# DeltaNet followed by soft MoE: the separate solve of the keys is taken out of each step, and the order is planned with other durations

## The chip, the cores and the metric

The kernel runs on one core of one Trainium2 chip. The metric is the device time of one execution in microseconds (us). A core has five engines that run beside each other, each through its own list of instructions in order: PE (TensorE, matrix products), DVE (VectorE), ACT (ScalarE), POOL (GpSimd) and SP (SyncE, which here only starts transfers). PE writes its results to PSUM, eight banks of 128 partitions by 512 floats; DVE and ACT bring them from there to SBUF.

## What is computed

The first half is a recurrent attention: for each of 4 x 8 pairs of batch and head, a state of 48 x 48 is carried through 768 positions. The second half routes the 3072 resulting rows through 8 experts with 4 slots each. Everything is float32.

```python
# attention: q, k, v (4, 8, 768, 48), beta (4, 8, 768)
k_n = k / (np.linalg.norm(k, axis=-1, keepdims=True) + 1e-06)
for t in range(S):
    y[:, :, t] = np.einsum('bhd,bhde->bhe', q[:, :, t], state)
    v_old = np.einsum('bhde,bhd->bhe', state, kt)
    state = state + bt[:, :, :, None] * np.einsum('bhd,bhe->bhde', kt, vt - v_old)
# soft MoE: x = y as (3072, 384), phi (384, 32), w1 (8, 384, 1024), w2 (8, 1024, 384)
logits = x @ phi
d = softmax of logits over the rows;  c = softmax of logits over the slots
slot_input = d.T @ x
h = np.maximum(slot_input[e] @ w1[e], 0.0);  slot_out[e] = h @ w2[e]
return c @ slot_out
```

## The kernel before, in words

The 768 positions are cut into 24 chunks ("steps", n = 0 to 23) of 32 positions; four batches of 32 positions fill the 128 partitions. Four steps make a group (m = 0 to 5). Inside a chunk the recurrence is a triangular system: with T the inverse of a unit lower triangular matrix built from the products of the chunk's keys, the chunk's update is W = T (V - K S), where S is the state on entry, K the keys and V the values.

Work that does not depend on the state, per group: loads of K, Q and V by SP; `turn` (L508, PE transposes of K and Q; ACT copies them to X at L518); `products` (L536, key by key and key by query; evicted to G at L549 and L553 and to AT at L557); `invert`, which makes T for the whole group (DVE transposes of 128x1024 at L574 and L670, 28 short POOL instructions at L653 and L657, two PE blocks at L701 and L706, and ACT's two scaled copies into DTb at L622); and `scale_v` (L725, POOL).

Work of one step, `chain(n)`, from step 1 on. One bank or pair of banks is taken for each product:

- KP, the solve of the keys (L755, PE, 16 products of 64x64): T K into two banks of the kind "bulk"; then an ACT copy of 128x512 with scale -1 (L764) overwrites the keys' half of X with it. It needs DTb and K, not the state.
- VP, the solve of the values (L773, PE): T V into two "chain" banks `hw`. It needs DTb, the scaled V and, by an explicit key, KP's copy, but not the state.
- R (L787, PE): -(T K) S is added to the same banks. It needs the state St.
- QS (L743, PE): Q S into a bank `hy`. It needs St.
- W: half of `hw` is spread into W by a DVE instruction (L799) and the other half by two of ACT (L804); ACT also makes the plain copy Wc (L808).
- S (L817, PE): K^T W is added to the state, which stays in two PSUM banks of its own; ACT (two of L827) and DVE (L831) copy it to St for the next step.
- AU (L842, PE) adds the chunk's inner part to `hy`, and ACT evicts it to Y (L848).

So the loop from state to state is R, W, S, St, and then R of the next step; KP and VP lie ahead of it.

After each group, `route` makes the logits and the running softmax sums (L866 to L950); after the last, `experts` runs the two expert layers (L1118, L1137, L1156) and the final product and stores (L1200 to L1220). The experts' weights are loaded by SP into the buffers of the first half as these come free (L1010). Rings of buffers: V has 6 slots, and SP's load of V for a later step (L476) waits until the last reader of the slot is done, which is VP of an earlier step.

The order in which each engine issues its work is written by a planner, `Plan`. Every `plan.op` gives an engine, a duration in us, what it reads and writes, and which PSUM banks it takes and frees. `order()` runs a list scheduling: at each moment it takes the operation of greatest worth, which is the length of the longest way to the end plus a correction by name from the table `BIAS` (the suffixes 0 and 5 stand for the first and last group). Six of the eight banks are shared; at most four may be held by "bulk" work. A model of the PE clock and of code fetching (`BLOCK`, `FETCH`) is part of it, and idle PE time may be filled with throw-away products (L466). The durations are estimates written in the code: `act(n)`, `dve(n)`, `pool(n)`, `pe(...)` or a plain number. The order is fixed when the program is made; on the chip each engine follows it and waits where something is late.

Of the kernel before, what the change touches and what calls it, by code (L numbers as in the profile page):

```python
# [10 lines left out]
ALU = mybir.AluOpType  # L11
ACT = mybir.ActivationFunctionType
# [5 lines left out]
    "ACT.DTb": 1.7, "ACT.DTb0": 0.8, "ACT.DTb5": -9.4, "ACT.G": 105.2, "ACT.G0": -5.0,  # L18
    "ACT.G5": 33.6, "ACT.Gl": 0.7, "ACT.Gl0": -20.9, "ACT.Gl5": -14.9, "ACT.KP": 3.6,
    "ACT.KP5": 56.7, "ACT.S": 17.6, "ACT.S5": 3.7, "ACT.W": -10.0, "ACT.W5": 13.1, "ACT.Wc":  # L20
    -4.6, "ACT.Wc5": 37.2, "ACT.X": -13.0, "ACT.X0": -8.8, "ACT.Y": 4.1, "ACT.Y5": 1.8,
    "ACT.al5": -6.7, "ACT.cT5": -37.8, "ACT.dT": 6.6, "ACT.gmax": 15.8, "ACT.hT": -23.0,
    "ACT.hr": 5.5, "ACT.lT5": 11.3, "ACT.norm": -15.2, "ACT.norm0": 21.2, "ACT.norm5": 5.9,
    "ACT.ob": 27.7, "ACT.share": -15.9, "ACT.share5": 2.6, "ACT.store": -8.0, "ACT.yT": 3.3,
    "ACT.yT5": -5.6, "DVE.AT": -15.1, "DVE.AT5": -27.5, "DVE.DT": -7.3, "DVE.DT-": 10.1,
    "DVE.DT-0": 23.8, "DVE.DT-5": -5.6, "DVE.DT0": -33.9, "DVE.DT5": -16.3, "DVE.DTb0": 60.8,
    "DVE.Dn5": 7.9, "DVE.G": -35.8, "DVE.G0": -2.5, "DVE.G5": 4.8, "DVE.N": -3.5, "DVE.N0":
    -14.4, "DVE.N5": 10.9, "DVE.S": 3.9, "DVE.S5": 24.7, "DVE.W": 4.4, "DVE.W5": -0.8,
    "DVE.X16": 17.4, "DVE.X160": -26.6, "DVE.X165": -14.0, "DVE.elim0": -28.1, "DVE.hT": 11.4,
    "DVE.lb": 86.8, "DVE.lb0": 35.6, "DVE.lb5": 14.0, "DVE.low0": 5.7, "DVE.low5": -18.5,  # L30
    "DVE.masks": -15.7, "DVE.max": 0.7, "DVE.max5": 13.4, "DVE.norm": 1.0, "DVE.norm0": -2.7,
    "DVE.norm5": -95.2, "DVE.ob": -6.6, "DVE.rd": 15.5, "DVE.sacc": 10.5, "DVE.sacc5": -13.5,
    "DVE.share5": -6.7, "DVE.sj": 5.0, "DVE.sl": -33.3, "DVE.so": -18.2, "DVE.ssq0": 32.2,
    "DVE.tD0": -62.5, "DVE.tS0": 3.1, "DVE.zero": 0.2, "PE.AU": -7.5, "PE.AU5": -5.2, "PE.KP":
    6.9, "PE.QS": -22.2, "PE.QS5": 3.8, "PE.R": -2.4, "PE.S": -0.1, "PE.S5": -14.4, "PE.T16":
    -9.8, "PE.T165": 12.8, "PE.VP": 8.8, "PE.VP5": 2.1, "PE.X16": 18.2, "PE.X160": -5.0,
    "PE.X165": -34.9, "PE.cT": -0.9, "PE.gather": 41.6, "PE.gmax": 1.1, "PE.logits": 14.4,
    "PE.logits5": 5.6, "PE.po": -0.1, "PE.prod": -5.8, "PE.prod0": -2.0, "PE.prod5": 3.0,
    "PE.second": 15.7, "PE.slots": 0.5, "PE.slots5": -4.4, "PE.turn": 4.5, "PE.turn0": -2.1,
    "PE.turn5": 33.5, "PE.turnD": 7.9, "PE.turnD5": 6.7, "PE.turnH": -15.5, "PE.turnL": 2.7,  # L40
    "PE.turnL5": 11.0, "PE.turnY": 42.7, "POOL.Dn2": 1.6, "POOL.Dn20": -6.1, "POOL.Dn25": 10.0,
    "POOL.elim": -6.7, "POOL.elim5": 0.8, "POOL.loadB0": 19.5, "POOL.loadP0": -10.4,
    "POOL.masks": 8.2, "POOL.one": 23.8, "POOL.one0": -19.4, "POOL.one5": 3.6, "POOL.scaleV":
    24.0, "POOL.scaleV5": 1.9, "POOL.share": -36.1, "POOL.share5": -22.5, "POOL.tD": -9.2,
    "POOL.tD5": -51.3, "POOL.tS": 20.2, "POOL.tS5": -4.9, "POOL.zero": 8.0, "SP.loadK0": 3.9,
    "SP.loadK5": 4.9, "SP.loadQ": -5.8, "SP.loadQ0": -88.6, "SP.loadV": -79.9, "SP.loadV0":
    43.4, "SP.loadV5": -4.8, "SP.loadW": 19.9, "SP.store": 4.3,
# [15 lines left out]
class Plan:  # L63
# [10 lines left out]
    BLOCK, FETCH, LAND = 128, 3.5, 2.3  # L74
# [240 lines left out]
def kernel(  # L315
# [39 lines left out]
    def buf(shape, name):  # L355
        return cpool.tile(shape, F32, name=name)
# [29 lines left out]
    Wc = [Wcall[:, i].rearrange("p (h d) -> p h d", d=D) for i in range(2)]  # L386
    St = buf([P, B, HQ, 2, D], "St")
# [24 lines left out]
    def act(n):  # L412
        return 0.22 + 0.00082 * n

    def dve(n, ps=False, per=1.04):
        return 0.035 + (0.15 if ps else 0.16) + n * per / 1000
# [106 lines left out]
    def products(n, which):  # L523
# [20 lines left out]
        for o, i in enumerate(which):  # L544
            ps = lambda o=o: at(h, 0, 2)[:, :, 0:2 * w * C * HQ].rearrange(
                "p g (e o t) -> p g e o t", e=HQ, o=w)[:, :, :, o, :]
            if i == 0:
                dst = G[m % 2][:, H * c:H * c + H].rearrange("p (e g) t -> p g e t", g=2)
                plan.op("ACT", act(256), lambda ps=ps, dst=dst: nc.scalar.activation(  # L549
                    dst, ps()[:, :, :, 0:C], ACT.Copy, scale=par[:, 0:1]), r=[h],  # L550
                    w=[("G", m % 2, c)], rel=h, name="G")
                for g in range(2):
                    D_(dve(128, True), lambda ps=ps, dst=dst, g=g: nc.vector.scalar_tensor_tensor(  # L553
                        dst[:, g], ps()[:, g, :, C:2 * C], par[:, 1:2], dst[:, g], op0=ALU.mult,
                        op1=ALU.add), r=[h, ("G", m % 2, c)], w=[("G", m % 2, c)], rel=h, name="G")
            else:
                D_(dve(512, True), lambda ps=ps: nc.vector.tensor_tensor(  # L557
                    AT[n % NA], ps(), tri.rearrange("p j t -> p (j t)").unsqueeze(1).unsqueeze(1)
                    .broadcast_to([P, 2, HQ, 2 * C]), op=ALU.mult),
                   r=[h], w=[("AT", n % NA)], rel=h, name="AT")  # L560
# [4 lines left out]
    def invert(m):  # L565
# [50 lines left out]
        for j in range(2):  # L616
# [4 lines left out]
            else:  # L621
                plan.op("ACT", act(1024) + 0.08, lambda j=j: nc.scalar.activation(  # L622
# [3 lines left out]
    def invert_joined(m, z, gr, gm, gk):  # L626
# [32 lines left out]
        for j in range(1, QC - 1):  # L659
            for part in range(2):  # L660
                n = 2 * j * (QC - 1 - j)
                plan.op(on, 0.31 + 1.72 * n / 1000 if m else dve(n, False, 0.86),
# [21 lines left out]
        for j in (1, 0):  # L684
            plan.op("POOL", 0.72, lambda j=j: nc.gpsimd.tensor_tensor(
# [3 lines left out]
        for j in range(2):  # L689
            plan.op("ACT", act(512), lambda j=j: nc.scalar.activation(  # L690
# [43 lines left out]
    def chain(n):  # L734
# [13 lines left out]
        hy, hw, hk = Banks(1, "chain"), Banks(2, "chain"), Banks(2, "bulk")  # L748
        if n:
            def solve_keys():  # L750
                for e in range(HQ):
                    for i in range(2):
                        for g in range(2):
                            rb = slice(2 * C * i, 2 * C * i + 2 * C)
                            nc.tensor.matmul(  # L755
                                at(hk, i)[DP * g:DP * g + DP, 2 * C * e:2 * C * e + 2 * C],
                                lhsT=kk[rb, 2 * e + g, :],
                                rhs=t[rb, H * c + 2 * e + g].rearrange("p j t -> p (j t)"),
                                start=(e == 0), stop=True, skip_group_check=True)

            plan.op("PE", pe(16, 64, 64, 4, 0.25), solve_keys,
                    r=[("DTb", m % 2, j) for j in range(2)] + all4("K", n % NK), w=[hk], acq=hk,
                    pre=[("X", n % NX, 0)], name="KP")
            plan.op("ACT", act(512), lambda: nc.scalar.activation(  # L764
                x[:, 0].rearrange("p e (i t) -> p i e t", i=2),
                at(hk, 0, 2)[:, :, 0:2 * C * HQ].rearrange("p i (e t) -> p i e t", e=HQ), ACT.Copy,
                scale=-1.0), r=[hk], w=[("X", n % NX, 0)], rel=hk, name="KP")

        def solve():
            for u in range(H):  # L770
                for i in range(2):
# [3 lines left out]
                                     rhs=vn[rb, u, :], start=(u % HQ == 0), stop=True,  # L775
# [3 lines left out]
                r=[("DTb", m % 2, j) for j in range(2)] + [("V", n % NV), ("X", n % NX, 0), "turns"],  # L779
                w=[hw], acq=hw, name="VP")  # L780
        if n:
            def shift():
                for e in range(HQ):
                    for b in range(B):
                        rb = slice(C * b, C * b + C)
                        e2 = 2 * D * (e % 2)
                        nc.tensor.matmul(at(hw, e // 2)[rb, e2:e2 + 2 * D], lhsT=x[:, 0, e, rb],  # L787
                                         rhs=St[:, b, e].rearrange("p g d -> p (g d)"),
                                         start=False, stop=True, skip_group_check=True)

            plan.op("PE", pe(16, 32, 96, 4, 0.25), shift,
                    r=[("X", n % NX, 0)] + sk, w=[hw, "turns"], bias=LOOP, name="R")
            plan.op("PE", pe(16, 32, 96, 4, 0.25), lambda: state(hy, 1),
                    r=[("X", n % NX, 1)] + sk, w=[hy], acq=hy, pre=[("Y", m % 2, c)], name="QS")

# [7 lines left out]
        for j in range(2):  # L803
            plan.op("ACT", act(192), lambda j=j: nc.scalar.activation(  # L804
# [53 lines left out]
    def route(m):  # L858
# [73 lines left out]
        plan.op("ACT", act(128), lambda: nc.scalar.activation(  # L932
# [94 lines left out]
    def experts():  # L1027
# [164 lines left out]
        for m in range(NG):  # L1192
# [14 lines left out]
            for s in range(2):  # L1207
# [8 lines left out]
                for x in range(2):  # L1216
# [3 lines left out]
                    plan.op(on, 0.5, lambda o=o, x=x, dst=dst, on=on: queues[on][0].dma_start(  # L1220
                            out=dst, in_=ob[o][0][DP * x:DP * x + DP]),
                        r=[("ob", o)], w=[("out", m, s, x)], land=0.55, name="store")
# [66 lines left out]
```

## Time and profile before

| | |
|---|---|
| median of 3 runs | 320.19 us (319.81 to 324.7) |
| profiled execution | 322.18 us; span of its trace 320.4 us |
| mean granted PE clock | 0.949 |
| PE / DVE / ACT / POOL busy | 273.6 / 167.0 / 156.5 / 107.0 us |
| PE busy from 44 to 274 us (windows view) | 210.0 of 230 us |
| KP: PE block L755, ACT copy L764 | 23 blocks, 17.1 us busy; 23 copies, 13.7 us busy |

The span is the time from the first to the last instruction of one profiled execution. It falls into three parts: up to about 44 us the first loads and the first group's inverse; from 44 to 274 us the steps, the other groups' inverses and the routing, all interleaved; from 274 us the experts and the stores. A row of the groups view gives the line, engine and shape of an instruction, how often it ran, its busy time, the mean duration of one, and how long its engine stood idle just before it. Each fp32 matrix product stands in the trace as two instructions, so a block of 16 products is 32 records. The records of neighbouring PE blocks overlap, since PE is pipelined; what a block occupies is read from its start to the start of the next. The chain of work goes back from the last instruction, at each step to what released it.

### The profile page before, as it was taken

The numbers are of one execution on the slowest core, as the hardware profiler recorded it, in microseconds if no ns is written. First come the engines' busy times: TensorE is split into PE (matmuls) and PEld (weight loads), VectorE is DVE, ScalarE is ACT, GpSimd is POOL, SyncE is SP. The second block draws the span as 40 slices with busy tenths as digits, with TensorE's granted clock in tenths as the row PEclk, the third lists the DMA queues.
The fourth block names the chain that finished last, engine by engine and source line by source line (L and its number), as shares of the span: only waits on it lengthen the run. The fifth ranks groups of instructions, "written<-read, shape, count | busy, mean of one in ns | idle before, by whom it ended". The sixth has DMA issues, their size and how long they took to land.

```text
span 320.4 us, 16406 instructions
## 1 busy us (share of the span) xinstructions
PE 273.6 (85%) x7296; PEld 223.1 (70%) x7296; DVE 167.0 (52%) x363; ACT 156.5 (49%) x325; POOL 107.0 (33%) x239
## 2 busy tenths in 40 slices
PE   3849797998997898999988999998898988999840
PEld 3739686887877797789867888787787875444410
DVE  7699992487345195445952648736231345220530
ACT  2542174637646357456485566853174765020330
POOL 9922148522872018830088400784000000000000
PEclk9987999899999799999999999999599999999995
DMA  5665544544444555544134660678677789595197
GB/s 96 101 108 83 96 79 72 92 66 77 78 73 83 85 86 86 81 69 79 23 91 88 126 210 5 166 179 304 222 210 239 219 256 359 162 407 202 50 302 237
DMA packets 88933, 45.25 MB, mean 141 GB/s; under 512 B 80016, under 2 KB 80144, under 8 KB 88864
## 3 DMA queue, kind: packets, MB, share of 16 engines
q1 hardware_dynamic: 86752, 42.69, 53.2%
q10 hardware_dynamic: 1568, 1.38, 1.4%
q8 instruction: 57, 0.93, 1.2%
q0 software_dynamic: 544, 0.15, 0.4%
q14 instruction: 12, 0.10, 0.1%
HBM read 39.47 MB, written 4.72 MB: 138 GB/s over the span
## 4 chain that ended last, share of the span: by engine, by line
PE 61%; DVE 14%; POOL 7%; issue 5%; DMA 5%; ACT 4%; SPq 0%; ACTq 0%; DVEq 0%; POOLq 0%
PE bank L842 7%; PE bank L536 6%; PE bank L743 5%; PE bank L773 5%; PE bank L817 5%; PE bank L787 5%; PE bank L508 4%; PE bank L755 3%; PE bank L1118 3%; PE bank L1156 3%; PE bank L701 3%; PE bank L706 3%; POOL bt L497 3%; PE bank L866 2%; DVE DT L670 2%
## 5 line engine op out<-in xcount | busy, mean ns | idle before, releaser
L518 ACT ACTIVATE X<-bank 128x512 f32<-128x512 f32 (+1 forms) x36 | 25.9, 739 | 32.1 <-PE bank L508 32.1
L725 POOL TENSOR_TENSOR Vall<-Vall,nT 128x384 f32<-128x384 f32 x24 | 19.8, 830 | 61.5 <-DMA Vall<-in_v_dram 29.9
L536 PE MATMUL bank<-X 48*64 48x64 f32 (+1 forms) x1152 | 32.9, 258 | 5.7 <-ACT X L518 5.3
L831 DVE TENSOR_TENSOR St<-bank,half 128x768 f32<-128x768 f32 x23 | 22.0, 955 | 26.3 <-PE bank L817 15.0
L536 PEld LDWEIGHTS bank<-X 48*64 48x64 f32 x1152 | 27.7, 149 | 10.5 <-ACT X L518 7.3
L827 ACT ACTIVATE St<-bank 48x384 f32<-48x384 f32 x46 | 22.3, 484 | 22.1 <-PE bank L817 12.9
L553 DVE SCALAR_TENSOR_TENSOR G<-bank,par,G 128x128 f32<-128x128 f32 x48 | 14.5, 342 | 28.4 <-ACT G L549 28.4
L773 PE MATMUL bank<-Vall,DTb 64*64 64x48 f32 x768 | 28.0, 222 | 0.6 <-issue 0.5
L842 PE MATMUL bank<-Wcall,ATall 64*64 64x48 f32 x768 | 27.6, 221 | 0.3 <-issue 0.3
L773 PEld LDWEIGHTS bank<-Vall,DTb 64*64 64x64 f32 x768 | 25.6, 138 | 3.2 <-issue 1.2
L842 PEld LDWEIGHTS bank<-Wcall,ATall 64*64 64x64 f32 x768 | 25.7, 138 | 1.7 <-issue 1.0
L657 POOL TENSOR_TENSOR tt<-tt,prPOOL 128x28 f32<-128x28 f32 (+6 forms) x70 | 24.7, 353 | 5.2
L804 ACT ACTIVATE W<-bank,par 128x192 f32<-128x192 f32 x48 | 17.5, 416 | 18.2 <-PE bank L787 17.4
L508 PE MATMUL bank<-ident,Kall 128*128 128x128 f32 x96 | 17.5, 319 | 9.5 <-DMA Kall<-in_k_dram 7.1
L653 POOL TENSOR_TENSOR prPOOL<-tt 128x28 f32<-128x28 f32 (+6 forms) x70 | 23.7, 339 | 5.0
L817 PE MATMUL bank<-W,Kall 64*48 64x96 f32 x736 | 22.6, 251 | 2.5 <-issue 1.9
L743 PE MATMUL bank<-St,X 128*32 128x96 f32 x736 | 22.7, 259 | 2.2 <-issue 1.6
L787 PE MATMUL bank<-St,X 128*32 128x96 f32 x736 | 20.8, 250 | 1.4 <-ACT St L827 0.8
L799 DVE TENSOR_TENSOR W<-bank,par 128x384 f32<-128x384 f32 x24 | 13.2, 550 | 15.9 <-PE bank L787 13.4
L817 PEld LDWEIGHTS bank<-W,Kall 64*48 64x48 f32 x736 | 17.5, 123 | 5.1 <-issue 3.4
L557 DVE TENSOR_TENSOR ATall<-bank,tri 128x512 f32<-128x512 f32 x24 | 16.4, 685 | 8.5 <-PE bank L536 8.1
L743 PEld LDWEIGHTS bank<-St,X 128*32 128x32 f32 x736 | 16.8, 114 | 5.6 <-issue 3.7
(212 smaller groups left out, 572.1 us busy)
## 6 DMA issues: line engine op xcount, KB each, us to landing
Vall<-in_v_dram SPq DMA_DIRECT2D x96, 48.0 KB, 2.6
Qall<-in_q_dram SPq DMA_DIRECT2D x96, 48.0 KB, 2.6
Kall<-in_k_dram SPq DMA_DIRECT2D x92, 48.0 KB, 2.5
X<-in_moe_w_dram SPq DMA_DIRECT2D x6, 512.0 KB, 4.6
X<-in_moe_w_dram SPq DMA_DIRECT2D x7, 384.0 KB, 5.6
Kall<-in_moe_w_dram SPq DMA_DIRECT2D x3, 512.0 KB, 5.0
Kall<-in_moe_w_dram SPq DMA_DIRECT2D x4, 384.0 KB, 5.6
ATall<-in_moe_w_dram SPq DMA_DIRECT2D x4, 384.0 KB, 5.5
```

The source lines that it names most:

```text
L508: nc.tensor.transpose(at(h, j)[:, P * e:P * e + P], src[:, P * e:P * e + P], ident)
L518: plan.op("ACT", act(512 * len(which)), lambda: nc.scalar.activation(dst, at(h, 0, 2) if len(which) > 1 else at(h).unsqueeze(1), ACT.Copy) ...
L536: nc.tensor.matmul(at(h, g)[rb, 2 * w * C * e:2 * w * C * (e + 1)], lhsT=x[r, 0, e, rb], rhs=x[r, which[0]:which[0] + w, e, rb], start=(e ...
L653: eng.tensor_tensor(o, t[:, :, j, 0:j].unsqueeze(2).broadcast_to([P, 2, w, j]), t[:, :, j + 1:QC, j].unsqueeze(3).broadcast_to([P, 2, w, j ...
L657: eng.tensor_tensor(t[:, :, j + 1:QC, 0:j], t[:, :, j + 1:QC, 0:j], o, op=ALU.add)
L743: nc.tensor.matmul(at(h)[rb, 2 * D * e:2 * D * e + 2 * D], lhsT=x[:, i, e, rb], rhs=St[:, b, e].rearrange("p g d -> p (g d)"), start=(e == ...
L773: nc.tensor.matmul(at(hw, u // HQ)[rb, D * (u % HQ):D * (u % HQ) + D], lhsT=t[rb, H * c + u].rearrange("p j t -> p (j t)"), rhs=vn[rb, u, ...
L787: nc.tensor.matmul(at(hw, e // 2)[rb, e2:e2 + 2 * D], lhsT=x[:, 0, e, rb], rhs=St[:, b, e].rearrange("p g d -> p (g d)"), start=False, sto ...
L817: nc.tensor.matmul(bank[DP * g:DP * g + D, SB + i, 0:H * D].rearrange("p (j e d) -> p e j d", j=2, e=HQ)[:, e], lhsT=kk[r, 2 * e + g, 0:D] ...
L827: plan.op("ACT", act(384), lambda r=r, g=g: nc.scalar.activation(St[r].rearrange("p (i j) e g d -> p i g (j e) d", i=2)[:, 0, g], bank[r, ...
L831: D_(dve(768, True), lambda: nc.vector.tensor_tensor(St.rearrange("p (i j) e g d -> p i (j e) g d", i=2)[:, 1], bank[:, SB + 1, 0:H * D].r ...
L842: nc.tensor.matmul(at(hy)[rb, D * u:D * u + D], lhsT=a[rb, u % 2, u // 2, :], rhs=wc[rb, u, :], start=(n == 0 and u == 0), stop=True, skip ...
```

## The change

Three things are changed.

1. In `chain(n)`, KP and its ACT copy are gone, so X keeps the plain keys. R now goes to a bank of its own, `hr`, first in the step; a new DVE instruction of 128x384 subtracts it from the scaled values into a new buffer R; QS follows in PE's program; and VP solves with that buffer as its right side. VP reads the buffer R and lists `hy`, so it comes after the subtraction and QS. In step 0 VP takes V as before. The key "turns", through which VP waited for the shift of the step before, is gone. There are no new or moved transfers in the code.
2. Durations that the planner uses are changed: `act`, `dve`, the elimination's instructions, some single copies, the code fetch (3.5 to 3.8) and the stores' landing (0.55 to 0.7).
3. The table `BIAS` is replaced: nearly every value differs, and so the planned order on every engine can differ.

```diff
 BIAS = {
...
-    BLOCK, FETCH, LAND = 128, 3.5, 2.3
+    BLOCK, FETCH, LAND = 128, 3.8, 2.3
...
+    R = buf([P, H, D], "R")
...
     def act(n):
-        return 0.22 + 0.00082 * n
+        return 0.185 + 0.00081 * n
 
     def dve(n, ps=False, per=1.04):
-        return 0.035 + (0.15 if ps else 0.16) + n * per / 1000
+        return 0.035 + 0.12 + n * per / 1000
...
-                plan.op(on, 0.31 + 1.72 * n / 1000 if m else dve(n, False, 0.86),
+                plan.op(on, 0.285 + 1.65 * n / 1000 if m else dve(n, False, 0.86),
...
-        hy, hw, hk = Banks(1, "chain"), Banks(2, "chain"), Banks(2, "bulk")
+        vk = [("V", n % NV)]
+        hy, hw = Banks(1, "chain"), Banks(2, "chain")
+        rhs = vn
         if n:
-            def solve_keys():
...
-            plan.op("PE", pe(16, 64, 64, 4, 0.25), solve_keys,
-                    r=[("DTb", m % 2, j) for j in range(2)] + all4("K", n % NK), w=[hk], acq=hk,
-                    pre=[("X", n % NX, 0)], name="KP")
-            plan.op("ACT", act(512), lambda: nc.scalar.activation(
-                x[:, 0].rearrange("p e (i t) -> p i e t", i=2),
-                at(hk, 0, 2)[:, :, 0:2 * C * HQ].rearrange("p i (e t) -> p i e t", e=HQ), ACT.Copy,
-                scale=-1.0), r=[hk], w=[("X", n % NX, 0)], rel=hk, name="KP")
+            hr = Banks(1, "chain")
+            rhs = R
+            plan.op("PE", pe(16, 32, 96, 4, 0.25), lambda: state(hr, 0),
+                    r=[("X", n % NX, 0)] + sk, w=[hr], acq=hr, bias=LOOP, name="R")
+            D_(dve(384, True), lambda: nc.vector.tensor_tensor(
+                R.rearrange("p u d -> p (u d)"), vn.rearrange("p u d -> p (u d)"),
+                at(hr)[:, 0:Dm], op=ALU.subtract), r=[hr] + vk, w=["R"], rel=hr, name="R")
+            plan.op("PE", pe(16, 32, 96, 4, 0.25), lambda: state(hy, 1),
+                    r=[("X", n % NX, 1)] + sk, w=[hy], acq=hy, pre=[("Y", m % 2, c)], name="QS")
 
         def solve():
...
-                                     rhs=vn[rb, u, :], start=(u % HQ == 0), stop=True,
+                                     rhs=rhs[rb, u, :], start=(u % HQ == 0), stop=True,
                                      skip_group_check=True)
 
         plan.op("PE", pe(16, 64, 48, 2, 0.25), solve,
-                r=[("DTb", m % 2, j) for j in range(2)] + [("V", n % NV), ("X", n % NX, 0), "turns"],
-                w=[hw], acq=hw, name="VP")
-        if n:
-            def shift():
...
-            plan.op("PE", pe(16, 32, 96, 4, 0.25), shift,
-                    r=[("X", n % NX, 0)] + sk, w=[hw, "turns"], bias=LOOP, name="R")
-            plan.op("PE", pe(16, 32, 96, 4, 0.25), lambda: state(hy, 1),
-                    r=[("X", n % NX, 1)] + sk, w=[hy], acq=hy, pre=[("Y", m % 2, c)], name="QS")
+                r=[("DTb", m % 2, j) for j in range(2)] + (["R", hy] if n else vk), w=[hw], acq=hw,
+                name="VP")
...
-                        r=[("ob", o)], w=[("out", m, s, x)], land=0.55, name="store")
+                        r=[("ob", o)], w=[("out", m, s, x)], land=0.7, name="store")
```

## The prediction, made before the result was known

> **What bounds the kernel now.** I read the page first, then the windows by stage, then the groups of the lines that change, and last the timeline of two steps. From the page:
>
> ```profile
> span 320.4 us, 16406 instructions
> PE 273.6 (85%) x7296; PEld 223.1 (70%) x7296; DVE 167.0 (52%) x363; ACT 156.5 (49%) x325; POOL 107.0 (33%) x239
> ...
> PE   3849797998997898999988999998898988999840
> ...
> PEclk9987999899999799999999999999599999999995
> ...
> PE 61%; DVE 14%; POOL 7%; issue 5%; DMA 5%; ACT 4%; SPq 0%; ACTq 0%; DVEq 0%; POOLq 0%
> ```
>
> PE is at eight to nine tenths nearly everywhere, the other engines are at about half, and the chain that ended last runs over PE for 61%. The windows view cuts the middle by the groups' inverses (columns: stretch, its length, PE, PEld, DVE, ACT and POOL busy, PE clock, DMA share, GB/s):
>
> ```profile
> 44.00:80.00 36.00, 32.12 (x1092) 28.39 (x1088) 22.09 (x44) 21.22 (x44) 18.10 (x43) 0.95 0.46 77
> 80.00:117.00 37.00, 33.27 (x951) 29.56 (x942) 16.51 (x27) 19.86 (x41) 15.69 (x33) 0.95 0.49 81
> 117.00:157.00 40.00, 37.98 (x1219) 33.23 (x1215) 23.25 (x47) 23.81 (x48) 16.90 (x38) 1.00 0.45 74
> 157.00:197.00 40.00, 37.31 (x1162) 32.69 (x1158) 23.24 (x49) 24.39 (x50) 17.24 (x39) 1.00 0.43 104
> 197.00:236.00 39.00, 34.77 (x1023) 30.07 (x1015) 18.65 (x40) 21.00 (x44) 17.36 (x39) 0.87 0.64 189
> 236.00:274.00 38.00, 34.50 (x978) 27.89 (x973) 15.38 (x46) 22.58 (x59) 1.60 (x4) 1.00 0.81 267
> ```
>
> PE is busy for 210.0 of these 230 us; no other engine reaches 25 of 40. So the middle is a matter of how much PE work there is, and of the 20 us in which PE waits. The groups that go, and the rows from which I price what comes:
>
> ```profile
> L755 PE MATMUL bank<-DTb,Kall 64*64 64x64 f32 x736 | 17.1, 224 | 2.1 <-issue 1.2 <-ACT Wcall L808 0.6
> L764 ACT ACTIVATE X<-bank 128x512 f32<-128x512 f32 x23 | 13.7, 598 | 8.0 <-PE bank L755 7.7
> L799 DVE TENSOR_TENSOR W<-bank,par 128x384 f32<-128x384 f32 x24 | 13.2, 550 | 15.9 <-PE bank L787 13.4 <-ACT Y L848 2.4
> ```
>
> The loop of the state, at its tightest place in the trace (the timeline, steps 4 and 5):
>
> ```profile
> 82.87 0.87 PE L787 MATMUL bank<-St,X 128*32 128x96 f32 x32
> 83.55 0.56 DVE L799 TENSOR_TENSOR W<-bank,par 128x384 f32<-128x384 f32 x1 [3.71 <-PE bank L787]
> 84.18 0.95 PE L817 MATMUL bank<-W,Kall 64*48 64x96 f32 x32
> 85.23 0.96 DVE L831 TENSOR_TENSOR St<-bank,half 128x768 f32<-128x768 f32 x1 [1.13 <-PE bank L817]
> 86.63 0.87 PE L787 MATMUL bank<-St,X 128*32 128x96 f32 x32
> ```
>
> From R to the next R it takes 3.76 us: 1.31 from R to S, 2.45 from S over St to R. But 23 steps have 230 us, 10 us each. The loop is far from the bound; PE is.
>
> **The change part by part.** *KP goes.* Its group is 17.1 us busy, but blocks overlap. Start to start in the timeline a KP block that isn't stalled takes 0.51 to 0.63 us (83.67 to 84.18, 87.59 to 88.22, 236.58 to 237.10). I take 0.6: 23 x 0.6 = 13.8 us off a PE that is the bound. The ends are 10.9 us (its 3.4% of the chain) and 17.1 us (all of its busy time). PE also issues 736 of 7296 products fewer, a tenth; the waits named "issue" are 5% of the chain, 16 us, so a tenth of these, 1.6 us, may go too: I take 0 and keep 1.6 for the lower end.
>
> *The ACT copy goes.* 13.7 us of an engine that is 49% busy. Its cover is PE. PE waited 5.3 us in all for ACT's copies to X at L518; up to that might be gained, I take 0.
>
> *The subtraction comes.* Like L799: 128x384 from PSUM on DVE, 0.55 us; 23 x 0.55 = 12.7 us brings DVE from 167 to 180 us, under 60%. Its place matters more than its sum.
>
> *VP and the subtraction enter the loop.* After R starts, an instruction that needs all of R starts 0.93 us later (254.99 to 255.90 and 259.88 to 260.81, ACT L804). Then 0.55 for the subtraction, 0.09 to PE (DVE's St ended at 91.57, R of step 6 started at 91.66): VP starts 1.57 us after R. QS (0.8 us) follows R (0.8 us), so PE works through this wait. From VP to S it takes 1.69 us, as in step 0, where VP alone makes W (43.10 to 44.79). So R to S becomes 3.26 instead of 1.31 us, and the loop 5.71 instead of 3.76. Where is that exposed? R to R, seven intervals of before are shorter than 5.71: 4.77, 3.76, 5.03, 4.95, 4.45, 5.59 and 4.89 us. They lack 6.5 us in all. Four of them lie before 140 us, where later intervals of 8 to 28 us make up for them. The last group (steps 20 to 23) has nothing behind it that could: there 4.45, 5.59 and 4.89 lack 2.2 us. I take 2.2; the ends are 0 (R of step 20 started at 244.95 although the state of step 19, whose S began at 237.10, should have been there 2.45 later, by 239.6, so the group can begin sooner) and 6.5.
>
> *VP waits for DVE.* PE is in order, so behind a late VP everything waits, the next group's transposes and products too. The worst companion is a DVE transpose of about 2 us (L574 and L670, 12 of them, 24.2 us). Scattered at random, a subtraction would meet one in a tenth of cases (24.2 of 230) and wait 1 us on average: 23 x 0.105 x 1.0 = 2.4 us. Both stand in the same planned DVE order, so it can do better: I take 0.6, ends 0 and 2.4.
>
> *Queues and buffers.* No transfer is added. A slot of V is now freed by the subtraction instead of VP, so SP's next loads of V, and the K, Q and weights behind them, may start later. That lies at most about 1.6 us behind the old moment where VP ran just ahead of R (steps 6 to 10). The row "SP waits for L773" has 27.2 us, but the values are also needed 1.6 us later, and POOL, which scales them, stands idle for two thirds of the span: 0; without that cover 1.6 us in each of the groups 1 to 4, about 6 us. In PSUM one bank `hr` is held from R to the subtraction's end, some 1.5 us, and two bulk banks are no longer held by KP: 0, ends -0.6 and 0.6 (one KP block either way).
>
> *Other durations, other BIAS.* They cost nothing themselves; they reorder every engine. What they can touch is the 20 us of PE waits in the middle and the stretches at half clock. The sign is open: 0, ends -3 and +5.
>
> Sum: -13.8 + 2.2 + 0.6 = -11.0 us. The profiled execution took 322.18 us, 1.8 more than its span, and is 2.0 us above the median; taken from it the sum gives 311.2, from the median of 320.19, which is what I forecast, **309 us**.
>
> **The clock, where the skill and the trace part.** In the windows view the granted clock drops to 0.50 in three stretches of the middle: 55.74 to 59.15, 106.94 to 110.35 and 222.99 to 233.23, 17.1 us. A stretch of 3.41 us at half clock does 1.7 us of work, so it costs 1.7 us.
>
> ```profile
> 102.00:106.94 4.94, 3.11 (x59) 2.39 (x54) 2.04 (x5) 2.54 (x5) 0.95 (x2) 1.00 0.57 94
> 106.94:110.35 3.41, 3.41 (x76) 3.13 (x72) 0.00 (x0) 1.15 (x2) 0.00 (x0) 0.50 0.43 73
> ```
>
> Before this one PE had been idle for 1.8 of 4.94 us, in waits of 0.43 and 1.40 us. So short waits are enough. The Trainium skill ("TensorE: Matmul & The Clock Gate", Part 1: The HAM clock gate) says that the clock falls after an idle window of about 3.4 us. By that rule no wait of the new loop, the longest about 1.5 us, could lower it, and the second rival below would have no chance; the trace contradicts it, and I go by the trace.
>
> **The rivals.** *First, the freed time comes back as waits (no change).* In the stages from 44 to 117 us the chain also holds transfers and POOL (Kall at 50.59, Vall at 78.99, POOL's tS at 91.93, Qall at 104.03); the six KPs there (3.6 us) may buy nothing. At least four later KPs (steps 9, 10, 13, 17) stood right behind R, where PE would have waited for W anyway: 2.4 us. With the loop at its 6.5 us and DVE's 0.6, the gain is 13.8 - 3.6 - 2.4 - 6.5 - 0.6 = 0.7 us: **319.5 us**. Against it: in the stages from 117 to 197 us PE waits only 4.7 of 80 us, with the same transfers and the same POOL work beside it, so there is other work to fill with.
>
> *Second, slower: the clock.* Before, VP and KP could be drawn ahead into waits; now each step leaves PE two waits, for W and for St (about 0.6 us, from VP's end to S, and 1.5 us, from S's end at 85.13 to R at 86.63), with only AU and work of other groups to fill them. If they stay open, the clock falls. Each stretch costs 1.7 us, so 7 more stretches eat the gain of 11, and 11 make it slower by over 2%. With 12, in every second step, it is 309.2 + 20.4 = **330 us**. For it: 1.8 us of idling sufficed at 106.94. Against it: three stretches in 230 us now, and about half of PE's work there lies outside the loop (L508, L536, L701, L706 and L866 are 102.6 of 210.0 us busy).
>
> **How the numbers follow.** Forecast 0.67 (its own range 301 to 314), no change 0.21, slower 0.12. A measurement of this kernel tells about 2% from no change, 6.4 us: under 313.8 is faster, over 326.6 slower. So faster 0.67, same 0.21, slower 0.12. The low end: 17.1 and 1.6 us gained and one stretch of half clock less, 320.2 - 17.1 - 1.6 - 1.7 = 299.8, say 300. The high end takes in the case of no change, 321; the slower case stays outside.
>
> **What would show it.** In the changed kernel's profile L755's and L764's groups should be missing, PE's busy time lower by 11 to 17 us, a DVE group of 23 at about 0.55 us stand between R and VP, VP start 1.6 us after R, and the tightest R to R be about 5.7 us. The stage up to 44 us and the 46 us from the first expert product on should stay as they are. I am wrong if PE's waits in the middle grow well beyond 20 us, if waits of VP for the subtraction add up to more than 3 us, or if the half-clock stretches grow by more than two.

## The result, and the profile after

The changed kernel takes 302.85 us (median of 4 runs, 300.48 to 306.08) against 322.44 us of the kernel before, run beside it (319.81 to 325.13). The ratio is 0.944, with a 95% interval from 0.925 to 0.962: faster by 19.6 us where 11 were forecast. The ratio leaves out executions in a slower state into which some runs of this kernel fall; by it the gain is 18 us. The profiled execution took 300.48 us, its span is 298.8 us. From the page of the changed kernel:

```profile
span 298.8 us, 14901 instructions
PE 256.3 (86%) x6540; PEld 208.1 (70%) x6540; DVE 180.5 (60%) x386; ACT 144.5 (48%) x302; POOL 108.5 (36%) x239
...
PE   3588699889999999999899999989778998999920
...
PEclk9967959989999999999999999999799999999995
...
PE 54%; DVE 16%; POOL 11%; ACT 6%; issue 6%; DMA 3%; ACTq 0%; DVEq 0%; SPq 0%; POOLq 0%
```

PE has 17.3 us less to do (11 to 17 were worked out), ACT 12.0 us less (13.7) and DVE 13.5 us more (12.7). PE is still the busiest engine, but the chain runs less over it (54% instead of 61%) and more over POOL, DVE and ACT. The windows view, cut at the first solve (49.28), at the same marks as before, and at the first expert product (252; columns as before):

```profile
0.00:49.28 49.28, 36.01 (x685) 31.91 (x685) 44.29 (x113) 19.33 (x36) 22.73 (x51) 0.83 0.56 95
49.28:80.00 30.72, 28.45 (x893) 25.46 (x892) 20.34 (x37) 15.91 (x35) 16.80 (x38) 0.94 0.47 78
80.00:117.00 37.00, 35.07 (x1047) 30.91 (x1049) 21.20 (x38) 21.89 (x46) 15.29 (x32) 1.00 0.48 82
117.00:157.00 40.00, 37.79 (x1160) 32.69 (x1153) 28.62 (x59) 24.70 (x52) 17.32 (x39) 1.00 0.47 79
157.00:197.00 40.00, 39.27 (x1155) 34.18 (x1152) 29.68 (x69) 27.73 (x60) 26.16 (x63) 1.00 0.59 159
197.00:236.00 39.00, 32.66 (x1014) 28.80 (x1013) 18.28 (x31) 18.22 (x43) 9.45 (x17) 0.96 0.77 263
236.00:252.00 16.00, 14.40 (x287) 10.73 (x280) 8.35 (x30) 8.90 (x25) 0.80 (x2) 1.00 0.85 281
```

The middle lasts 203 us instead of 231 (from the first solve at 43.1 to the first expert product at 273.9). PE is busy for 187.6 us of it, 23 us less than the 210.9 of before (43 to 274 us), and idle for 15 instead of 20. The granted clock is at half in it for 6.8 us instead of 17.1, which is 5 us of work. The tail is as it was, 47 us. Against this, the first solve starts 6.2 us later. Ahead of it the half clock covers 17.1 us (13.6 to 20.5, 23.9 to 27.3 and 37.5 to 44.4) instead of 6.8 (21.6 to 28.4), so up to the first expert product it is 23.9 us before as after. DVE is busy there for 44.3 of 49.3 us (37.2 of 43.1 before), and its instructions at L645 and L612 for the next group now run ahead of its last two for the first group's inverse (L722 at 47.01, L621 at 47.74). Which of these makes the first solve late was not tested.

The new step, in the timeline of step 5 (some rows between these are left out; state product and QS share line L746; subtraction L759, solve L769, S L798, AU L823):

```profile
87.10 1.53 PE L746 MATMUL bank<-St,X 128*32 128x96 f32 x64 [0.22 <-ACT St L808]
88.19 0.55 DVE L759 TENSOR_TENSOR R<-Vall,bank 128x384 f32<-128x384 f32 x1 [1.18 <-DMA Qall<-in_q_dram]
88.89 1.14 PE L769 MATMUL bank<-R,DTb 64*64 64x48 f32 x32 [0.26 <-DVE R L759]
90.98 0.88 PE L798 MATMUL bank<-W,Kall 64*48 64x96 f32 x32
91.68 1.10 PE L823 MATMUL bank<-Wcall,ATall 64*64 64x48 f32 x32
```

The solve starts 1.79 us after R (1.54 at step 6; 1.57 was worked out), QS lies between, and PE waits 0.26 us for the subtraction. In the other steps further work of PE can stand between R and the solve. The shortest intervals from R to R are 5.45, 5.58 and 5.79 us; 5.71 was worked out for the tightest loop.

### The profile page after: what moved, and what is told of

The parts are those of the page before. It is cut to its first block, busy times and chain, and to the rows that moved or that the text cites. A ratio compares the mean times of both kernels' runs of the same rounds, so it can differ in the third digit from the quotient of the medians.

```text
span 298.8 us, 14901 instructions
## 1 busy us (share of the span) xinstructions
PE 256.3 (86%) x6540; PEld 208.1 (70%) x6540; DVE 180.5 (60%) x386; ACT 144.5 (48%) x302; POOL 108.5 (36%) x239
## 4 chain that ended last, share of the span: by engine, by line
PE 54%; DVE 16%; POOL 11%; ACT 6%; issue 6%; DMA 3%; ACTq 0%; DVEq 0%; SPq 0%; POOLq 0%
PE bank L746 8%; PE bank L769 7%; PE bank L539 5%; PE bank L798 5%; PE bank L704 4%; PE bank L823 4%; PE bank L1099 4%; PE bank L1137 4%; POOL prPOOL L656 3%; POOL tt L660 3%; PE bank L511 3%; ACT St L808 3%; POOL bt L500 3%; PE bank L709 3%; DVE DT L673 2%
## 5 line engine op out<-in xcount | busy, mean ns | idle before, releaser
L746 PE MATMUL bank<-St,X 128*32 128x96 f32 x1472 | 39.4, 253 | 6.1 <-issue 3.6
L746 PEld LDWEIGHTS bank<-St,X 128*32 128x32 f32 x1472 | 31.9, 112 | 11.8 <-issue 6.2
L521 ACT ACTIVATE X<-bank 128x512 f32<-128x512 f32 (+1 forms) x36 | 26.4, 740 | 13.6 <-PE bank L511 13.5
L769 PE MATMUL bank<-R,DTb 64*64 64x48 f32 x736 | 27.5, 225 | 4.1 <-issue 1.4
L769 PEld LDWEIGHTS bank<-R,DTb 64*64 64x64 f32 x736 | 24.8, 140 | 8.3 <-issue 3.1
L823 PE MATMUL bank<-Wcall,ATall 64*64 64x48 f32 x768 | 27.1, 218 | 0.7 <-issue 0.7
L656 POOL TENSOR_TENSOR prPOOL<-tt 128x28 f32<-128x28 f32 (+6 forms) x70 | 24.8, 355 | 5.1
L823 PEld LDWEIGHTS bank<-Wcall,ATall 64*64 64x64 f32 x768 | 25.3, 135 | 1.8 <-issue 0.9
L552 ACT ACTIVATE G<-bank,par 128x256 f32<-128x256 f32 x24 | 11.4, 475 | 19.8 <-PE bank L539 19.7
L759 DVE TENSOR_TENSOR R<-Vall,bank 128x384 f32<-128x384 f32 x23 | 12.7, 550 | 13.6 <-PE bank L746 7.3
L798 PE MATMUL bank<-W,Kall 64*48 64x96 f32 x736 | 20.8, 247 | 0.0
L798 PEld LDWEIGHTS bank<-W,Kall 64*48 64x48 f32 x736 | 16.3, 119 | 4.0 <-issue 2.4
```

What stands on the lines that cost most here:

```text
L521: plan.op("ACT", act(512 * len(which)), lambda: nc.scalar.activation(dst, at(h, 0, 2) if len(which) > 1 else at(h).unsqueeze(1), ACT.Copy) ...
L656: eng.tensor_tensor(o, t[:, :, j, 0:j].unsqueeze(2).broadcast_to([P, 2, w, j]), t[:, :, j + 1:QC, j].unsqueeze(3).broadcast_to([P, 2, w, j ...
L746: nc.tensor.matmul(at(h)[rb, 2 * D * e:2 * D * e + 2 * D], lhsT=x[:, i, e, rb], rhs=St[:, b, e].rearrange("p g d -> p (g d)"), start=(e == ...
L769: nc.tensor.matmul(at(hw, u // HQ)[rb, D * (u % HQ):D * (u % HQ) + D], lhsT=t[rb, H * c + u].rearrange("p j t -> p (j t)"), rhs=rhs[rb, u, ...
L798: nc.tensor.matmul(bank[DP * g:DP * g + D, SB + i, 0:H * D].rearrange("p (j e d) -> p e j d", j=2, e=HQ)[:, e], lhsT=kk[r, 2 * e + g, 0:D] ...
L823: nc.tensor.matmul(at(hy)[rb, D * u:D * u + D], lhsT=a[rb, u % 2, u // 2, :], rhs=wc[rb, u, :], start=(n == 0 and u == 0), stop=True, skip ...
```

## The experiments

My theory: PE is the bound, so the gain is the PE time of the keys' solve, and the longer loop is hidden. Rivals: the gain is the new order (durations and corrections), or the loop binds. Beside the first group of runs the changed kernel was run again.

> The changed kernel unaltered, beside the other three on the same chip: 300 to 306 us; the differences of the other three are taken from this one.

It took 303.75 us, ratio 0.941 (0.934 to 0.949), as expected. Differences below are taken from 303.3, the mean of its two medians.

**The keys' solve put back into the new order.** The first form stood ahead of AU:

```diff
         def inner():
+            for e in range(HQ if n else 0):
+                for i in range(2):
+                    for g in range(2):
+                        rb = slice(2 * C * i, 2 * C * i + 2 * C)
+                        nc.tensor.matmul(
+                            bank[DP * g:DP * g + DP, SB + i, Dm + 32:Dm + 32 + 2 * C],
+                            lhsT=kk[rb, 2 * e + g, :],
+                            rhs=t[rb, H * c + 2 * e + g].rearrange("p j t -> p (j t)"),
+                            start=False, stop=True, skip_group_check=True)
             for u in range(H):
```

> The changed kernel in its own order, with the 16 products of the keys' solve put back into PE's program ahead of each step's AU, into unused PSUM columns that nothing reads (no ACT copy, and the planner does not know of them). Theory (PE is the bound, the gain is the PE time of these blocks): 0.52 to 0.67 us for each of 23 blocks, so 12 to 15.4 us above the changed kernel, 313 to 318 us. Rival (the gain is the new order; PE waits about 23 us anyway and such a block fits into a wait): 0 to 5 us, 301 to 307 us.

338.7 us (ratio 1.054, 1.044 to 1.065), 35 us above, and so beyond both. The waits view says why (line, what it waited for, total us, times, longest):

```profile
PE bank L824 <- DMA Kall<-in_k_dram: 12.1, 8, 5.1
...
PE bank L824 <- DMA Kall<-in_moe_w_dram: 3.9, 1, 3.9
```

By the time of AU the slot of K had been given to a later load, so the block waited for transfers. This run doesn't price PE work. The second form stands behind S, where the slot is still held (the added products are the same nine lines):

```diff
         def update():
...
                             lhsT=kk[r, 2 * e + g, 0:D], rhs=ww[r, 2 * e + g],
                             start=(n == 0 and e == 0), stop=True, skip_group_check=True)
+            for e in range(HQ if n else 0):
...
```

> The run that put KP's products back ahead of AU measured something else: by then SP had already been told to load a later chunk's keys into the same slot of K, and PE waited for that load (16 us of named waits on Kall). Here the 16 products stand right behind S, which reads the same slot, so no load is involved; the rest of the changed kernel's order is as it is. Theory (a block of PE work costs its PE time): 0.52 to 0.67 us for each of 22 blocks, 11.4 to 14.7 us above the changed kernel (302.85 and 303.75), 314 to 318 us. Rival (PE stands idle there for the state, 1.5 us from the end of S to R, and the block hides in it): 0 to 4 us, 303 to 307 us.

312.68 us (ratio 0.975, 0.968 to 0.981): 9.4 us above by the medians, 10 to 11 by the ratios, or about 0.45 us for each of 22 blocks. That is below the 0.52 to 0.67 of the theory, and far above the rival's 4. The timelines say why it is less. Step 6 in the changed kernel, and the same step with the added block (L807; AU is L832 there):

```profile
100.00 0.88 PE L798 MATMUL bank<-W,Kall 64*48 64x96 f32 x32
100.69 1.02 PE L823 MATMUL bank<-Wcall,ATall 64*64 64x48 f32 x29
```

```profile
101.81 0.88 PE L798 MATMUL bank<-W,Kall 64*48 64x96 f32 x32
102.51 0.64 PE L807 MATMUL bank<-DTb,Kall 64*64 64x64 f32 x32
102.98 1.02 PE L832 MATMUL bank<-Wcall,ATall 64*64 64x48 f32 x29
```

From S to what follows it takes 0.69 us without the block and 1.17 with it; over all 22 steps, 16.6 and 26.7 us, or 0.46 us for a block. PE's idle time in the middle did not shrink (16.0 us, in the changed kernel 15.1), so the blocks were not hidden in waits: in this place a block simply occupies PE for less than 0.6 us. All of it is paid. So in the new order KP's products are worth about 10 us; in the order of before, where blocks that weren't stalled took 0.51 to 0.63 us, they may have taken up to the 13.8 us of the forecast.

**Does the loop bind?** Again the first form was flawed:

```diff
-            rhs = R
+            rhs = vn
```

> The changed kernel in its own order, but the solve reads the scaled values themselves: the state product and the subtraction are still carried out and nothing needs their result, so the state no longer enters the solve and the output is not the reference's. Theory (the longer loop is hidden): no more than 3 us below the changed kernel, 298 to 303 us. Rival (the loop bounds the steps): 12 of the 22 intervals from R to R are under 7.4 us; if each shrank by the 2 us that the subtraction and the solve add, 24 us below, about 278 us.

353.43 us (ratio 1.095, 1.084 to 1.105), slower by 50 us although a dependence was taken out:

```profile
PE bank L769 <- DMA Vall<-in_v_dram: 25.2, 12, 5.0
PE bank L769 <- DMA Vall<-in_moe_w_dram: 6.9, 2, 3.7
```

In the planned order the slot of V is reloaded behind the subtraction, and a solve that reads the slot after that waits for the load. The mean clock fell to 0.882. With a constant in place of the slot:

```diff
+    Rc = buf([P, H, D], "Rc")
+    nc.vector.memset(Rc, 0.05)
...
-            rhs = R
+            rhs = Rc
```

> The run in which VP read the scaled values had the same flaw: VP then waited for later loads into the same slot of V (32 us of named waits). Here the solve reads a buffer that is filled once with a constant, so it needs neither R nor the subtraction; both are still carried out, in the changed kernel's order, and the output is not the reference's. Theory (the longer loop is hidden in the tuned order): 0 to 3 us below the changed kernel, 300 to 304 us. Rival (the loop bounds many steps): the 12 intervals from R to R under 7.4 us shrink by up to 1.5 us where nothing else stands in PE's program, 10 to 18 us below, 285 to 294 us.

301.64 us (ratio 0.940, 0.934 to 0.946), 1.7 us below the changed kernel by the medians and 0.1 to 0.4% by the ratios, as the theory had it. In this order the longer loop costs nothing that these runs can tell, and not the rival's 10 to 18 us; a cost of 2 us lies within their noise.

**A slower subtraction.**

```diff
-            D_(dve(384, True), lambda: nc.vector.tensor_tensor(
+            D_(dve(384, True), lambda: [nc.vector.tensor_tensor(
                 R.rearrange("p u d -> p (u d)"), vn.rearrange("p u d -> p (u d)"),
-                at(hr)[:, 0:Dm], op=ALU.subtract), r=[hr] + vk, w=["R"], rel=hr, name="R")
+                at(hr)[:, 0:Dm], op=ALU.subtract) for _ in (0, 1)], r=[hr] + vk, w=["R"], rel=hr, name="R")
```

> The changed kernel in its own order with every subtraction carried out twice, 0.55 us more of DVE in each of 23 steps. The prediction had QS cover the subtraction almost to the end (VP 1.57 us after R, QS ending 1.6 us after R). If that is so, every step whose VP directly follows QS in PE's program (about 14) now holds PE for 0.5 us: about 7 us above the changed kernel, 308 to 311 us. Rival (there is slack between QS and VP): 0 to 2 us, 301 to 305 us. If the loop were the bound everywhere: 13 us, 314 us.

307.58 us (ratio 0.956, 0.948 to 0.964): 4.3 us above, between the two expectations. PE's wait for the subtraction, 1.1 us in all in the changed kernel, grew to 7.8:

```profile
PE bank L769 <- DVE R L759: 7.8, 11, 0.9
```

So the wait falls on PE 11 times; it grew by 6.7 us and the time by 4.3, so about a third of it is made up for later.

**Step and order apart.** The changed step under the tables of before, and the step of before under the new ones (each file is one kernel with the other's `chain` up to the solve):

> The kernel before with only the changed step (no KP, state product and subtraction ahead of the solve); durations and table of corrections as before. Theory (the gain is PE work taken out, whatever the order): 12 to 16 us below the kernel before, 304 to 309 us. Rival (the gain is the new order): the old corrections do not fit the changed step, 315 to 325 us.

348.52 us (ratio 1.074, 1.062 to 1.086), 24 us above the kernel before by the ratio, 26 by the medians.

> The step of the kernel before (with KP) under the changed kernel's durations and table of corrections. Theory: PE has all its work again, so no faster than the kernel before, 318 to 326 us. Rival (the order brings most of the gain): 305 to 312 us.

346.71 us (ratio 1.081, 1.071 to 1.090). Both are slower than either kernel, and both theory and rival missed: neither half brings anything alone. Then both steps without corrections (`BIAS = {}`), under the new durations:

> The step of the kernel before (with KP), the new durations, and no corrections at all: an order that is tuned for neither. Theory: some 5 to 15 us above the kernel before for the lost tuning, 325 to 335 us; what counts is the distance to the next one.

331.99 us (ratio 1.031, 1.024 to 1.038), within what was expected.

> The changed step, the new durations, and no corrections. Theory: 12 to 16 us below the run with KP and no corrections. Rival (the longer loop needs the tuned order): less than 5 us below it, or above.

354.75 us (ratio 1.091, 1.080 to 1.102): with an order made for neither, the changed step is 19 us (by the ratios) to 23 us **slower**. My theory "whatever the order" fell with these four. One place where these orders lose time is seen in SP's waits. First the step with KP, then the changed step (here L786 and L765 are S, L742 the solve; L445 and L446 the loads of K, Q and V):

```profile
SPq L445 <- PE bank L742: 20.9, 8, 5.8
...
SPq L445 <- PE bank L786: 6.5, 7, 3.4
```

```profile
SPq L446 <- PE bank L765: 32.8, 8, 12.9
```

S is the last reader of a slot of K. In the changed step's run SP waits 32.8 us for it, five times as long; with KP it waits longest for the solve, the last reader of a slot of V. PE's own waits name loads less often: in the middle of this run PE stands idle for 30 us and under the tables of before for 38 us, of which DVE ends 14 and 25 us and transfers 6 and 2. So that late loads of K make these orders slow is argued here and not shown. From the timelines: a group's products and its inverse come behind its K transposes, and POOL's elimination between them takes 12 to 14 us in all of these kernels (once 18):

| | K transposes of groups 2 to 5 start their last at, us | last inverse ready | first expert product |
|---|---|---|---|
| before | 59, 105, 148, 185 | 234 | 273.9 |
| changed | 68, 108, 146, 173 | 212 | 251.8 |
| with KP, no corrections | 73, 114, 152, 192 | 244 | 281.3 |
| changed step, no corrections | 68, 128, 186, 227 | 269 | 297.8 |
| changed step, tables of before | 61, 124, 172, 214 | 262 | 293.1 |

In the two bad orders of the changed step a group comes every 41 to 63 us, in the changed kernel every 27 to 40. In the run without corrections the planner fills holes with 88 throw-away products, against 6 with KP (37 in the kernel before, 27 in the changed one).

Last, both steps with a table of equal making:

```diff
-BIAS = {}
+BIAS = {
...
+}
```

The tables are those with the shortest planned end among 2 x 3000 random tries for each step, from the empty table on.

> The step with KP, the new durations, and a table of corrections found from an empty one by a search of two times 3000 tries for the shortest planned order. It and the next run differ in the step alone and had the same search. Theory: the search takes back the 10 us that the empty table cost, 318 to 325 us. Rival (the planned order says little about the chip): 328 to 335 us, as with no corrections.

333.99 us (ratio 1.033, 1.025 to 1.042): the rival's range. The planned end had come down from 323 to 312 us, the chip's time did not.

> The changed step, the new durations, and a table found by the same search from an empty one. Theory (the step is worth 10 to 15 us less PE time once the order is made for it): 10 to 16 us below the run with KP and a searched table, 303 to 312 us. Rival (the step is worth nothing by itself, and the changed kernel's gain comes from one fortunate table): no better than the run with KP and a searched table, 318 to 330 us.

314.81 us (ratio 0.978, 0.971 to 0.985): planned 296 after 359, and 40 us shorter on the chip than with the empty table. It is 18 to 19 us below the other step with an equally made table, more than the 10 to 16 of the theory, and some 2% below the kernel before, though not as fast as the changed kernel. All medians in us, with the end that the planner itself gives for each file in brackets:

| | tables of before | new tables | empty | searched |
|---|---|---|---|---|
| step with KP | 322.4 (302) | 346.7 (361) | 332.0 (323) | 334.0 (312) |
| changed step | 348.5 (335) | 302.9 (293) | 354.8 (359) | 314.8 (296) |

The first column is planned with the durations of before, the others with the new ones. Both orders that were carried over to the other step, and the changed step with the empty table, are bad in the plan already: their planned ends lie 33 to 68 us above those of the two kernels.

## Why the prediction was right, and where it was not

The direction and its main reason held: PE is the bound of the middle, and less PE work shortens it. The time, 302.85, lies in the range of 300 to 321, and in the forecast's own of 301 to 314; the forecast of 309 gave 11 us where 18 to 19.6 came. That it lies in the range is in part luck: the low end of 300 was reached by taking KP at all of its busy time, 17.1 us, and not by a better order. By its terms:

- **KP's PE time, -13.8 us.** About -10 by the run with the products behind S, near the end of 10.9 taken from the chain: a block occupies 0.46 us there and not 0.6. In the order of before -13.8 may hold. The trace of that run, in which the blocks stand behind S, shows none that hides in a wait, as the first rival had some do behind R.
- **The longer loop, +2.2.** Not measurable (solve with a constant, ratio 0.940 against 0.941 and 0.944); these runs can't tell 2 us from nothing. The working of the loop itself, 5.71 us, was right to 0.3 us at its shortest, 5.45.
- **The wait for the subtraction, +0.6.** PE's named wait is 1.1 us. Right in size; doubling the subtraction costs 4.3.
- **Other durations and corrections, 0 with ends -3 and +5.** This is the step that failed. With -10 to -13.8 for KP and about +1 for the rest, some 5 to 10 us of the gain are left. This is a difference and not a measurement, and it also contains whatever the ACT copy and KP's two banks were worth, which no run prices apart (PE's named waits for ACT in the middle are 4 us before and 3 after). In the profile there is 5 us less idling in the middle and 5 us less of half clock (10.3 us at half speed), and more PE work went ahead of the first solve; the head, 6.2 us longer and with 10.3 us more at half clock, takes part of it back. And the order can do far more harm than +5: 42 to 46 us between the changed kernel and the same step under the tables of before. I had called the order neutral because no row prices it; the step and its order were one change.
- **Slots of V freed later, 0.** The place was right and the ring was the wrong one: in the bad orders SP waits most for slots of K, which S frees at the end of the now longer step. This is read from waits, and PE's own waits there are mostly for DVE; a run with more slots of K was not tried, so it isn't shown that they make those orders slow.
- **The head stays.** Wrong: the first solve starts at 49.3 instead of 43.1 us. This comes with the order: the changed step under the tables of before starts it at 44.2 us, the step of before under the new ones at 51.3.

Waits that eat the gain, as the first rival had them, are what happens under the tables of before: PE idles for 38 us of the middle there instead of 20. The second rival, the clock, did not come in the middle: 6.8 us at half clock. One argument against it was misread: the 102.6 us of work outside the loop are sums over the whole kernel, and from 44 to 274 us these lines have 78 of the 210 us, not about half. The searched tables show that the changed step is worth about as much (18 to 19 us) in an order that was searched afresh, one search for each step, so the gain isn't one fortunate table. Why the search helped one step on the chip and not the other stays open.

## What to carry to other kernels

Where a planner or a hand-made order is tuned to a kernel, a change of the dependences is not worth what its instructions cost: here the same edit was worth -18 to -20 us in its own order, about the same in an order searched afresh, and +19 to +26 in orders not made for it. Where the planner gives an end of its own, read it before the chip: here it told the two kernels from the bad orders, though it missed by up to 22 us and did not foretell the searched step with KP. Price the removed work on the engine that binds, and then ask what the new dependence does to the release of buffers, since loads for the next stage wait there. To price a block by putting it back, put it where all that it reads is still held; otherwise the run measures a wait for a later load.

## What the runs showed of the hardware

A fall to half clock can follow a single short wait of PE; the prediction's row had two, of 0.43 and 1.40 us. In the changed kernel one wait of 0.91 us (for DVE, ahead of L704) in a stretch of 3.41 us was followed by a stretch at 0.50 (columns as above):

```profile
61.42:64.83 3.41, 2.50 (x92) 2.43 (x92) 3.09 (x6) 0.47 (x1) 0.90 (x2) 1.00 0.58 94
64.83:68.25 3.42, 3.42 (x56) 2.77 (x45) 1.22 (x3) 0.87 (x3) 1.36 (x3) 0.50 0.42 67
```

PE was busy for 2.50 of the 3.41 us before the fall, mostly with products of 32 columns (L704). A wait of 0.71 us ahead of the same line, up to 93.48 us, was not followed by one. In the run whose solves read a constant, a wait of 2.50 us up to 109.42 us was not followed by one either. So the length of a wait alone doesn't decide it, and these runs don't show what does. The Trainium skill's rule of an idle window of about 3.4 us ("TensorE: Matmul & The Clock Gate", Part 1: The HAM clock gate) doesn't agree with the two lines above either. In the run whose solves waited for later loads of V, waits of up to 5.0 us, the mean clock was 0.882 against 0.941 of the changed kernel beside it.
